# Pair 3's transposes moved from the matrix engine to the DMA queue, two others put ahead of stores, in a fused retention and bilinear feed-forward kernel

## The chip, the cores and the metric

The kernel runs on one core of one Trainium2 chip. The metric is the device time of one execution in microseconds (us). Times are medians over several executions, and each kernel is compared with the kernel before in runs on the same chip in the same batch. Only one execution of one experiment fell in the chip's "slow" state (named where it happens); all comparisons use fast runs.

## The reference

Two stages. First, retention (linear attention with a decay) over 8 batches, 8 heads, 576 positions and a head size of 64. Then a bilinear feed-forward on the 4608 tokens.

```python
scores = scale * np.matmul(q, k.transpose(0, 1, 3, 2))
gamma = 1.0 - 2.0 ** (-5.0 - np.arange(H))
Dmat = np.where(rel >= 0, gamma[:, None, None] ** rel, 0.0)
x = np.matmul(scores * Dmat, v)            # then (B, S, H*D) -> (4608, 512)
out = ((x @ w_a) * (x @ w_b)) @ w_out      # 512 -> 1536 -> 512
```

## The kernel before

The kernel interleaves the two stages by hand. The feed-forward runs in blocks of tokens: block 0 has 512, blocks 1 and 2 have 256, all others 512. Between its products a list called `todo` starts the pieces of the attention that a later block needs; the number in front is a place in the stream of products, counted in products of 512 columns. From the seventh 128-row tile on, the attention works on "pairs" of tiles (256 tokens), numbered 3 to 17: pair 3 is the first. A pair goes through these steps: `load_pair` (DMA in), `ahead` (GpSimd casts to bf16), a transpose of queries and keys, and a "stretch", in which TensorE makes the states (`kv`), the scores (`sc`) and the outputs (`o`).

All loads, all stores and all DMA transposes are issued by one engine, SyncE, in program order:

```python
def load_pair(n, which=(0, 1, 2)):
    ...
            nc.sync.dma_start(...)                 # two issues for each of q, k, v

def turn(n):                                       # transposes of a pair by DMA
    qkb = of(natural, n)[0]
    qkT = qkt_pool.tile([128, 2, 2, HP, 128], BF16, tag="qkT", name="qkT2")
    for w in (0, 1):                               # queries, then keys
        nc.sync.dma_start_transpose(
            qkT[:, w].rearrange("p k c s -> p (k c) s"), qkb[:, w])
    ...

def turned(n, part):                               # the same on TensorE, pair 3 only
    ...
    tp = ps_ffn.tile([128, HP, 128], BF16, tag="ab", name="tp2")
    for c in range(HP):                            # 4 transposes; called 4 times
        nc.tensor.transpose(tp[:, c, :], qkb[:, w, e0:e0 + 128], identity)
    copy = (nc.scalar.copy, nc.vector.tensor_copy)[kp]
    copy(of(transposed, n)[:, w, kp], tp)
```

The output of a block leaves through one of four SBUF buffers (`osb`). Blocks 1 and 2 have all their output copies on ScalarE, the same engine that copies `pa` out of PSUM and converts the states:

```python
o_pool = pool("osb", 4)
...
for u in range(n // 128):                          # in ffn_block(tb, tok0, n, runs)
    osb = o_pool.tile([128, DM], FP32, tag="osb", name="osb")
    ...                                            # po = hT x wo_sb, 12 products
    elif n == 256 or (u + part) % 2 == 0:
        nc.scalar.copy(osb[:, cols], po[:, 0:width])
    ...
    store(tok0 // 128 + u, cols, osb)              # nc.sync.dma_start
    pop()                                          # runs one deferred piece of work
```

The deferred pieces (`later`) are taken up one at a time by `pop()`, at fixed points of the feed-forward. They mask the scores and add the state sums on VectorE, and convert the states to bf16 on ScalarE. The schedule, as far as it matters here:

```python
warm(8, 512)                                       # fillers at the start
...
for n in (FIRST, FIRST + 1):                       # FIRST = 3
    load_pair(n)
load_pair(FIRST + 2, (Q, K))
...
todo += [(170, stretch, (3, None)), (197, stretch, (4, 3)),
         (236, stretch, (5, 4)), (266, open_alone, (5,)), ...
casts = {3: 116, 4: 116, 5: 141, 6: 200, 7: 250, 8: 330}
turns = {4: 116, 5: 145, 6: 240, 7: 338, 8: 345}
todo += [(156 + 3 * part, turned, (3, part)) for part in range(4)]
todo += [(116, load_pair, (5, (V,)))]
```

Of the kernel before, what the change touches and what calls it, by code (L numbers as in the profile page):

```python
# [10 lines left out]
FP32 = mybir.dt.float32  # L11
BF16 = mybir.dt.bfloat16
# [6 lines left out]
def kernel(  # L19
# [10 lines left out]
    nc = tc.nc  # L30

    B, H, S, D = q.shape
    DM = H * D
# [4 lines left out]
    HP = H // 2  # L38
# [8 lines left out]
    FIRST = 3  # L47
# [27 lines left out]
    qkt_pool = pool("qkt", 3)  # L75
# [46 lines left out]
    def half(i):  # L122
        return slice(64 * i, 64 * i + 64)
# [37 lines left out]
    Q, K, V = 0, 1, 2  # L161
# [311 lines left out]
            op=ALU.mult)  # L473
        natural[FIRST + n, "pair"] = (qkb, vb)

    def turned(n, part):

        qkb = of(natural, n)[0]
        if part == 0:
            transposed[FIRST + n, "pair"] = qkt_pool.tile(  # L480
                [128, 2, 2, HP, 128], BF16, tag="qkT", name="qkT2")
        w, kp = part // 2, part % 2
        tp = ps_ffn.tile([128, HP, 128], BF16, tag="ab", name="tp2")
        for c in range(HP):
            e0 = kp * DM + c * 128
            nc.tensor.transpose(tp[:, c, :], qkb[:, w, e0:e0 + 128], identity)
        copy = (nc.scalar.copy, nc.vector.tensor_copy)[kp]
        copy(of(transposed, n)[:, w, kp], tp)

    def turn(n):  # L490
        qkb = of(natural, n)[0]
        qkT = qkt_pool.tile([128, 2, 2, HP, 128], BF16, tag="qkT",
# [8 lines left out]
    def of(store, n):  # L501
        return store[FIRST + n, "pair"]
# [179 lines left out]
    def store(u, cols, osb):  # L682
        n, u = place(u // 2), u % 2
        for kp, r0, m, b, s0 in rows_of(n):
            rows = out[b * S + s0:b * S + s0 + m, cols]
            if kp != u:
                continue
            if n < FIRST:
                for par in (0, 1):
                    nc.sync.dma_start(rows[par::2], osb[half(par), cols])  # L690
            else:
                nc.sync.dma_start(rows, osb[r0:r0 + m, cols])

    begun = {}

    def ffn_begin(F):
# [13 lines left out]
    def ffn_block(tb, tok0, n, runs):  # L710
# [42 lines left out]
        for u in range(n // 128):  # L753
            final = tok0 + (u + 1) * 128 == NTOK
            osb = o_pool.tile([128, DM], FP32, tag="osb", name="osb")
            for part in range(2 if final else 1):
                cols = (slice(part * DM // 2, (part + 1) * DM // 2) if final
                        else slice(0, DM))
                po = ps_ffn.tile([128, 512], FP32, tag="ab", name="po")
                width = cols.stop - cols.start  # L760
                for F in range(NF):
                    nc.tensor.matmul(po[:, 0:width],  # L762
                                     hT[:, F, u * 128:(u + 1) * 128],
                                     wo_sb[:, F, cols],
                                     start=(F == 0), stop=(F == NF - 1))
                    if F in (2, 5, 8):
                        pop()
                    if F < NF - 1:
                        yield width / 512, F % 4 == 3
                if part:  # L770
                    mid = (cols.start + cols.stop) // 2
                    nc.scalar.copy(osb[:, cols.start:mid],
                                   po[:, 0:width // 2])
                    nc.vector.tensor_copy(osb[:, mid:cols.stop],
                                          po[:, width // 2:width])
                elif n == 256 or (u + part) % 2 == 0:
                    nc.scalar.copy(osb[:, cols], po[:, 0:width])  # L777
                else:
                    nc.vector.tensor_copy(osb[:, cols], po[:, 0:width])  # L779
                store(tok0 // 128 + u, cols, osb)  # L780
                pop()
                yield width / 512, True

# [4 lines left out]
    def warm(count, n):  # L788

        w = ps_ffn.tile([128, 512], FP32, tag="ab", name="w")  # L790
        for _ in range(count):
            nc.tensor.matmul(w[:, 0:n], ones[:, 0:128], ones[:, 0:n],  # L792
                             start=True, stop=True)

    W1, W2 = 128 * WCOLS[0], 128 * (WCOLS[0] + WCOLS[1])
    vector, pool_ = nc.vector, nc.gpsimd
    warm(8, 512)
    make_qs(qs_o, 0, 0, 512)
    for i in range(4):
        place_step(i)  # L800
# [67 lines left out]
        load_step(*STEPS[i], which)  # L868
    for n in (FIRST, FIRST + 1):
        load_pair(n)  # L870
    load_pair(FIRST + 2, (Q, K))



# [30 lines left out]
    def turn_step(i):  # L905
# [8 lines left out]
            (140, output_step, (5,))]  # L914
    todo += [(28 + 6 * step, pair_tables, (step,)) for step in range(13)]
    todo += [(170, stretch, (3, None)), (197, stretch, (4, 3)),
             (236, stretch, (5, 4)), (266, open_alone, (5,)),
             (270, close_outputs, (5,)), (336, stretch, (6, None)),
             (372, stretch, (7, 6)), (408, stretch, (8, 7))]
    for n in range(8, NP, 2):  # L920
# [4 lines left out]
    todo += [(starts[NP - 2] - 40, close_outputs, (NP - 1,))]  # L925
    placed = {args[0]: at for at, fn, args in todo if fn is stretch}
    casts = {3: 116, 4: 116, 5: 141, 6: 200, 7: 250, 8: 330}
    turns = {4: 116, 5: 145, 6: 240, 7: 338, 8: 345}
    loads = {7: 212, 8: 271, 9: 345.1, 10: 345.2}
    todo += [(145.1, load_pair, (6, (K,))),  # L930
             (145.2, load_pair, (6, (Q,))), (145.3, load_pair, (6, (V,)))]
    for n in range(9, NP):
        casts[n], turns[n] = placed[n] - 70, placed[n] - 38
    todo += [(156 + 3 * part, turned, (3, part)) for part in range(4)]
    for fn, places in ((ahead, casts), (turn, turns), (load_pair, loads)):
        todo += [(at, fn, (n,)) for n, at in places.items()]
    todo += [(116, load_pair, (5, (V,)))]
    todo.sort(key=lambda e: e[0])

    at = 0.0  # L940
# [40 lines left out]
```

## Time and profile before

| | before |
|---|---|
| time, first three runs | 330.65 us median (329.9 to 331.17) |
| span of the profiled execution | 328.6 us |
| TensorE busy | 322.2 us, 98% |
| granted clock, profiled execution | 1.000 |
| first product of block 0 / 1 / 2 / 3 | 17.69 / 52.86 / 71.52 / 90.45 us |

With an engine that is busy for 98% of the span, the useful question is not "how busy is it" but "where does it stand still, and for what". The last row of the table is the moments at which TensorE starts the first product of each block. (Line numbers: the scores are L587 in the kernel before and L573 in the changed one; the other lines shift likewise.)

### The profile page before, as it was taken

Reading aid. Unit: us, or ns where it says so; the run is one execution under the profiler, and the core shown is the slowest. Engines: PE = TensorE matmul, PEld = TensorE weight load, DVE = VectorE, ACT = ScalarE, POOL = GpSimd, SP = SyncE. Lnnn points to the kernel's source line nnn. Section 1 sums busy time; section 2 is a strip of 40 time slices with the busy share of each in tenths; the row PEclk is TensorE's granted clock in tenths of the full one; section 3 lists DMA queues with packets and bytes.
Section 4 is the critical chain, followed back from the end, with each engine's and each line's share of the span. In section 5 each row is a group of like instructions: output and inputs, shape, how many; then the busy total and the mean of one; then the engine's idle time right before and its main releaser. Section 6 shows DMA issues by size and latency. Waiting matters only on the chain.

```text
span 328.6 us, 8735 instructions
## 1 busy us (share of the span) xinstructions
PE 322.2 (98%) x3658; PEld 168.9 (51%) x3658; DVE 162.5 (49%) x291; ACT 128.9 (39%) x277; POOL 114.5 (35%) x146
## 2 busy tenths in 40 slices
PE   8999999999999999999999999999999999999995
PEld 4664467867544554545454545454445444444443
DVE  6744445665536673745274626562456245414421
ACT  7734743553435424533244323531333333213321
POOL 3960069820867185644074305360520000000000
PEclk9999999999999999999999999999999999999999
DMA  7999999989999999991799068935850510031013
GB/s 214 253 184 207 258 229 216 186 197 194 221 227 244 199 209 248 219 215 55 178 215 202 35 151 203 193 100 132 184 101 16 143 38 0 2 96 34 1 32 96
DMA packets 143175, 50.37 MB, mean 153 GB/s; under 512 B 124576, under 2 KB 138656, under 8 KB 143136
## 3 DMA queue, kind: packets, MB, share of 16 engines
q1 hardware_dynamic: 138384, 45.10, 62.8%
q0 software_dynamic: 4752, 4.72, 8.9%
q8 instruction: 28, 0.46, 0.6%
q14 instruction: 11, 0.09, 0.1%
HBM read 37.75 MB, written 9.44 MB: 144 GB/s over the span
## 4 chain that ended last, share of the span: by engine, by line
PE 92%; DMA 2%; POOL 2%; DVE 1%; SPq 1%; issue 1%; ACT 1%; POOLq 0%; ACTq 0%; DVEq 0%
PE po L762 27%; PE pb L743 27%; PE pa L728 26%; PE w L792 2%; PE o L613 1%; PE o L626 1%; DMA vf<-in_v_dram 1%; PE sc L587 1%; PE kv L360 1%; DMA qkT<-qkb 1%; PE kv L530 1%; PE tp L316 1%; PE pa L705 1%; PE o L421 1%; PE sc L331 1%
## 5 line engine op out<-in xcount | busy, mean ns | idle before, releaser
L748 DVE TENSOR_TENSOR hT<-ha,pb 128x512 bf16<-128x512 bf16 (+1 forms) x120 | 75.8, 633 | 99.1 <-PE pb L743 93.4
L736 ACT CAST ha<-pa 128x512 bf16<-128x512 f32 (+1 forms) x120 | 64.8, 542 | 120.4 <-PE pa L728 116.6
L743 PE MATMUL pb<-xT,wb_sb 128*128 128x512 bf16 (+1 forms) x480 | 111.5, 358 | 0.1
L728 PE MATMUL pa<-xT,wa_sb 128*128 128x512 bf16 (+1 forms) x468 | 108.8, 357 | 0.0
L762 PE MATMUL po<-wo_sb,hT 128*128 128x512 bf16 (+1 forms) x444 | 97.5, 374 | 0.4 <-issue 0.4
L743 PEld LDWEIGHTS <-wb_sb 128*128 128x128 bf16 x480 | 46.9, 98 | 46.6 <-issue 0.3
L728 PEld LDWEIGHTS <-wa_sb 128*128 128x128 bf16 x468 | 44.9, 98 | 44.3 <-issue 0.2
L762 PEld LDWEIGHTS <-hT 128*128 128x128 bf16 x444 | 42.2, 98 | 47.2 <-issue 0.5
L464 POOL CAST qkb<-qf 64x1024 bf16<-64x1024 f32 x15 | 15.4, 1030 | 82.8 <-DMA qf<-in_q_dram 80.6
L469 POOL TENSOR_TENSOR vb<-vf,vs 128x1024 bf16<-128x1024 f32 x15 | 28.5, 1901 | 11.7 <-DMA vf<-in_v_dram 8.7
L779 DVE COPY osb<-po 128x512 f32<-128x512 f32 (+1 forms) x16 | 10.8, 674 | 39.5 <-PE po L762 39.5
L777 ACT COPY osb<-po 128x512 f32<-128x512 f32 x20 | 11.7, 585 | 44.9 <-PE po L762 44.6
L636 DVE TENSOR_TENSOR xT<-o,qs 128x512 bf16<-128x512 f32 x30 | 19.5, 683 | 4.4 <-PE o L626 4.4
L550 DVE TENSOR_TENSOR sums<-kv,sums 128x256 f32<-128x256 f32 x46 | 19.5, 424 | 2.8 <-PE kv L530 0.8
L596 DVE TENSOR_TENSOR sT<-sc,mask 128x512 bf16<-128x512 f32 x30 | 19.5, 682 | 0.0
L468 POOL CAST qkb<-kf 64x512 bf16<-64x512 f32 x30 | 17.6, 614 | 0.9
L468 POOL CAST qkb<-qf 64x512 bf16<-64x512 f32 x30 | 17.6, 614 | 0.6
L464 POOL CAST qkb<-kf 64x1024 bf16<-64x1024 f32 x15 | 15.5, 1033 | 6.0 <-DMA kf<-in_k_dram 5.7
L554 ACT CAST states<-sums 64x512 bf16<-64x512 f32 x26 | 16.0, 617 | 0.3
L299 POOL CAST qkb<-kf 128x512 bf16<-128x512 f32 x5 | 3.1, 613 | 19.1 <-DMA kf<-in_k_dram 19.1
L792 PE MATMUL w<-ones 128*128 128x256 bf16 (+1 forms) x34 | 7.9, 361 | 1.5 <-DVE ones L197 1.5
L653 ACT COPY fence<-o 128x2 f32<-128x2 f32 x15 | 2.4, 161 | 15.8 <-PE o L613 15.8
(83 smaller groups left out, 163.0 us busy)
## 6 DMA issues: line engine op xcount, KB each, us to landing
qf<-in_q_dram SPq DMA_DIRECT2D x32, 256.0 KB, 4.8
kf<-in_k_dram SPq DMA_DIRECT2D x32, 256.0 KB, 5.2
vf<-in_v_dram SPq DMA_DIRECT2D x32, 256.0 KB, 5.2
out_dram<-osb SPq DMA_DIRECT2D x25, 256.0 KB, 2.2
out_dram<-osb SPq DMA_DIRECT2D x22, 128.0 KB, 2.4
wo_sb<-in_moe_w_out_dram POOLq DMA_DIRECT2D x3, 512.0 KB, 16.8
qf<-in_q_dram SPq DMA_DIRECT2D x8, 128.0 KB, 3.4
kf<-in_k_dram SPq DMA_DIRECT2D x8, 128.0 KB, 3.5
```

Source lines behind the costliest of these rows:

```text
L464: nc.gpsimd.tensor_copy(qkb[0:64, w], t[0:64])
L468: nc.gpsimd.tensor_copy(to[:, :, 1 - r], fro[:, :, r])
L469: nc.gpsimd.tensor_tensor(vb.rearrange("p (k h d) -> p k h d", k=2, h=H), vf.rearrange("p (k h d) -> p k h d", k=2, h=H), vs2[:, 2 if n in ...
L550: nc.vector.tensor_tensor(sums[:, i], own, prev, op=ALU.add)
L554: nc.scalar.copy(to(half(1 - r)), fro(half(r)))
L596: nc.vector.tensor_tensor(sT[:, on].rearrange("p c k s -> p (c k) s"), sc[:, on].rearrange("p c k s -> p (c k) s"), mask3.unsqueeze(1).to_ ...
L636: nc.vector.tensor_tensor(x_of(t0, 128).rearrange("p c (a s) -> p c a s", a=2), o[:, :, :, kp].rearrange("p a c s -> p c a s"), qs[:, :, s ...
L728: nc.tensor.matmul(pa[:, 0:n], wa_sb[:, c, fs], xT[:, c], start=(c == 0), stop=(c == NC - 1))
L736: nc.scalar.copy(ha[:, 0:n], pa[:, 0:n])
L743: nc.tensor.matmul(pb[:, 0:n], wb_sb[:, c, fs], xT[:, c], start=(c == 0), stop=(c == NC - 1))
L748: nc.vector.tensor_tensor(hT[:, F, 0:n], has[F][:, 0:n], pb[:, 0:n], op=ALU.mult)
L762: nc.tensor.matmul(po[:, 0:width], hT[:, F, u * 128:(u + 1) * 128], wo_sb[:, F, cols], start=(F == 0), stop=(F == NF - 1))
```

## The change

The intent is to take sixteen transposes out of TensorE's stream by giving pair 3's to the DMA queue, as all other pairs' are, and to have the transposes of pairs 4 and 5 issued before stores that nobody waits for. The stretch of pair 5 moves four products on, and 48 short fillers on two quadrants of the array take the place of three long ones at the start. The diff, cut:

```diff
-    def turned(n, part):
-        ...
+    held = []
+
+    def store_held():
+        while held:
+            store(*held.pop(0))
...
-                store(tok0 // 128 + u, cols, osb)
+                if tb == 0 and u > 1:
+                    held.append((u, cols, osb))
+                else:
+                    store(tok0 // 128 + u, cols, osb)
...
+    def warm_quads(count):          # 64-column matmuls on 64 x 64 quadrants in turn
+        ...
-    warm(8, 512)
+    for _ in range(3):
+        warm_quads(16)
+    warm(5, 512)
...
-    load_pair(FIRST + 2, (Q, K))
...
-             (236, stretch, (5, 4)), (266, open_alone, (5,)),
+             (240, stretch, (5, 4)), (266, open_alone, (5,)),
...
-    turns = {4: 116, 5: 145, 6: 240, 7: 338, 8: 345}
+    turns = {5: 145, 6: 240, 7: 338, 8: 345}
...
-    todo += [(156 + 3 * part, turned, (3, part)) for part in range(4)]
...
-    todo += [(116, load_pair, (5, (V,)))]
+    todo += [(116, turn, (3,)), (116, load_pair, (5, (Q,))),
+             (116, turn, (4,)), (116, load_pair, (5, (K, V))),
+             (145, store_held, ())]
```

More of the change, by code (lines that the diff above doesn't have):

```diff
@@ L474, in ahead @@
         natural[FIRST + n, "pair"] = (qkb, vb)
-    def turned(n, part):
-        qkb = of(natural, n)[0]
-        if part == 0:
-            transposed[FIRST + n, "pair"] = qkt_pool.tile(
-                [128, 2, 2, HP, 128], BF16, tag="qkT", name="qkT2")
-        w, kp = part // 2, part % 2
-        tp = ps_ffn.tile([128, HP, 128], BF16, tag="ab", name="tp2")
-        for c in range(HP):
-            e0 = kp * DM + c * 128
-            nc.tensor.transpose(tp[:, c, :], qkb[:, w, e0:e0 + 128], identity)
-        copy = (nc.scalar.copy, nc.vector.tensor_copy)[kp]
-        copy(of(transposed, n)[:, w, kp], tp)
     def turn(n):
@@ L793, in warm @@
                              start=True, stop=True)
+    def warm_quads(count):
+        w = ps_ffn.tile([128, 512], FP32, tag="ab", name="w4")
+        for i in range(count):
+            r = i % 2
+            nc.tensor.matmul(w[half(r), 0:64], ones[half(r), 0:64],
+                             ones[half(r), 0:64], start=True, stop=True)
     W1, W2 = 128 * WCOLS[0], 128 * (WCOLS[0] + WCOLS[1])
     vector, pool_ = nc.vector, nc.gpsimd
-    warm(8, 512)
+    for _ in range(3):
+        warm_quads(16)
+    warm(5, 512)
     make_qs(qs_o, 0, 0, 512)
```

## The prediction

> **What bounds the kernel now.** I read the page's busy shares first, then the chain of work that ended last, then TensorE's timeline between 53 and 81 us, the SyncE queue's timeline over the same stretch, and last the first 6 us.
>
> ```profile
> PE 322.2 (98%) x3658; PEld 168.9 (51%) x3658; DVE 162.5 (49%) x291; ACT 128.9 (39%) x277; POOL 114.5 (35%) x146
> PE 92%; DMA 2%; POOL 2%; DVE 1%; SPq 1%; issue 1%; ACT 1%; POOLq 0%; ACTq 0%; DVEq 0%
> ```
>
> TensorE is busy all the time and is 92% of the chain. So a saving counts only if it takes work or a wait out of TensorE's own stream, and TensorE executes its instructions in order: a wait in front of one matmul holds all that follow. The 8% that are not TensorE lie in the first 18 us and in one place near 77 us:
>
> ```profile
> 66.01 4.25 DMA vf<-in_v_dram
> ...
> 70.48 1.91 POOL vb L469
> 72.40 1.10 SPq L495
> ...
> 73.60 3.29 DMA qkT<-qkb
> ...
> 76.93 0.45 PE sc L587 x32
> ```
>
> Columns: start, length, what. The scores of pair 5 (L587) waited for a transpose by DMA, issued at 73.60 and landed 3.29 us later. The matmuls before it (L530, 32 at about 11.6 ns each) started at 76.23, so without the wait the scores would have started at about 76.5. It costs about 0.4 us. After it TensorE slips by another 0.6 us in the next four products (78.0 to 80.4), where VectorE has the state sums to add between its products and the four PSUM buffers are taken.
>
> The part that the change removes, in TensorE's timeline (start, length, what; overlapping lengths include the pipeline, so I go by starts):
>
> ```profile
> 57.67 0.39 PE L486 MATMUL tp<-identity,qkb 128*128 128x128 bf16 x4
> 57.90 0.60 PE L728 MATMUL pa<-xT,wa_sb 128*128 128x256 bf16 x4
> ...
> 59.96 0.45 PE L530 MATMUL kv<-vb,qkb 64*64 64x64 bf16 x32
> 60.23 0.44 PE L587 MATMUL sc<-qkT 64*64 64x64 bf16 x32
> 60.60 0.61 PE L728 MATMUL pa<-xT,wa_sb 128*128 128x256 bf16 x4
> ```
>
> A group of four transposes delays the next product by 0.22 us. The scores of pair 3 start at 60.23 with nothing to wait for, only 1.5 us after the last transpose.
>
> The SyncE queue, which issues every load, store and transpose in program order:
>
> ```profile
> 51.91 2.09 SPq L142 DMA_DIRECT2D vf<-in_v_dram  x2
> 54.10 2.49 SPq L142 DMA_DIRECT2D qf<-in_q_dram  x2
> 56.69 3.23 SPq L142 DMA_DIRECT2D kf<-in_k_dram  x2
> 60.02 0.74 SPq L690 DMA_DIRECT2D out_dram<-osb  x1
> ...
> 61.51 3.82 SPq L495 DMA_TRANSPOSE qkT<-qkb  x2
> 65.38 1.25 SPq L142 DMA_DIRECT2D vf<-in_v_dram  x2
> 66.74 5.35 SPq L690 DMA_DIRECT2D out_dram<-osb  x6
> 72.19 2.67 SPq L495 DMA_TRANSPOSE qkT<-qkb  x2
> ```
>
> It goes from issue to issue without a pause from 33 us on, about 1.1 us for each 256 KB load, and the page shows the DMA engines at nine tenths there. The queue is full: what stands in it lands some 4 to 6 us after its issue. Whoever puts a transfer on this queue has to look at when the queue gets to it.
>
> The start:
>
> ```profile
> 1.52 3.59 PE L792 MATMUL w<-ones 128*128 128x512 bf16 x8 [1.52 <-DVE ones L197]
> ...
> 4.91 1.06 PE L316 MATMUL tp<-identity,qkb 128*128 128x128 bf16 x8
> ```
>
> Eight fillers take 0.43 us each, twice the 0.216 us of the same size later on; the first transposes start when they end.
>
> **What the Trainium skill says.** (1) "TensorE: Matmul & The Clock Gate", Part 1: the clock stays at half until a free-running window of about 3.4 us has been busy. The trace agrees: fillers from 1.52 us run at half rate, the 256-column ones at 5.76 come down to 0.109 us. Since the window doesn't start with the kernel, the moment of the grant is partly chance. (2) Same page, Part 4: a transpose on TensorE lands in PSUM and needs a copy, and costs about 275 ns in a kernel. The copies are here (585 ns on ScalarE, 418 on VectorE), but the cost isn't: 0.22 us for four, 55 ns each. The measurement decides. (3) "DMA: Bandwidth & Descriptors", "Queues, rings and completion order": on each DMA engine descriptors are consumed in ring order. The trace agrees: landings on this queue follow the order of issue. (4) Same page, "Rules for kernel authors": a transpose next to ordinary DMAs needs nothing, so no extra wait is put between them.
>
> **The change part by part.**
>
> Pair 3 off TensorE. Sixteen transposes at 55 ns: 16 x 0.055 = 0.88 us less in TensorE's stream, all on the path. Two copies each on ScalarE and VectorE go too, in stretches where neither is late: nothing.
>
> Pair 3 onto the queue. The loads up to pair 4's values end their issue at 54.0 as before. Pair 5's queries and keys no longer follow; the first block's first store does: two issues of 0.69, 54.1 to 55.5. Then pair 3's transposes: queries 55.5 to 56.9, keys from 57.0. Their sources are long cast (GpSimd finished pair 3's keys at 51.4). Landing: pair 4's transpose, issued in the same place behind the same loads and stores, took 4.6 us from issue (61.51 to about 66.1). So the keys land at 57.0 + 4.6 = 61.6. TensorE, 0.88 us earlier, is at these scores at 60.23 - 0.88 = 59.35, for the stretch of pair 3 is left where it was. It must wait 61.6 - 59.35, about 2.2 us. This is the term I trust to decide the sign: 0.88 saved, 2.2 given back, so +1.35 net at this point.
>
> Pairs 4 and 5 ahead of stores. From 58.3: pair 5's queries (2.3) to 60.6, pair 4's transposes (2.7) to 63.3, landed by about 67; needed at 67.39 + 1.35 = 68.7: no wait. Then pair 5's keys and values (4.2) to 67.5, one store pair to 68.8, transpose of the queries to 70.2. The keys land at about 70, their casts take 1.03 + 1.17, so the second transpose is issued at about 72.2 and lands at about 75.5. Pair 5's stretch, four products (4 x 0.216 = 0.86 us) later and 1.35 us later from above, is at its scores at about 76.5 + 2.2 = 78.7. The wait of 0.4 us goes: -0.4. Half of this would have come from either part alone. The four products are only moved, not removed: 0. The sums that hold up TensorE by 0.6 us stand behind the stretch in the new place too, so I count 0.
>
> Fillers. Three of eight fillers (3 x 0.43 = 1.3 us) become 48 of 64 columns on two quadrants of the array in turn. On four quadrants at full clock the trace has 11.6 ns each (32 in 0.37 us), so on two about 23, at half clock up to 46: 1.1 to 2.2 us. The first transposes are between 0.2 us earlier and 0.9 later. What arrives by DMA at 7 to 14 us in the start sets much of the rest. Above all, whatever the start gives or costs up to about 2 us is swallowed by the wait at pair 3's scores, which ends by the DMA queue's clock. So 0.
>
> Sum: 330.65 - 0.88 + 2.2 - 0.4 = 331.6. I shade it to 331.4, since the landing is the soft number and has more room to be earlier than later.
>
> **Rivals.** (a) The transposes land sooner: two loads fewer stand in the queue, and where it wasn't full a transpose took 3.3 us. Then the keys land at 60.3, the wait is 0.95, and the sum is 330.3: no change. The full landing row (median 3.4 over all 28) speaks for it, the nine-tenths DMA at 54 to 62 us against it. (b) They land before 59.35: then the change saves 1.3 us, 329.3. It would need a latency of 2.3 us; I saw none so short. (c) The fillers matter: the clock comes a whole window later because short matmuls on half the array don't count as busy. Then up to 3.4 us run at half rate, 1.7 us lost, of which the wait at pair 3 hides most; at worst about 332.5. (d) The two added transposes (2.6 us of issue) push the whole queue back, and the later pairs wait: pair 7's last transpose landed at about 107.7 and is needed at 110.85, so 3 us of slack cover it, barely. If it doesn't, +0.3.
>
> **Range and chances.** The three runs before spread from 329.9 to 331.17, half a us either way. With the landing between 60.3 and 62.0 the sum runs from 330.3 to 332.0; with the scatter and the fillers I say 329.9 to 332.8. Two per cent is 6.6 us, and no part is that large in either direction: within 2% almost for sure, faster 0.01, slower 0.02.
>
> **What would show it.** In the chain of waits or TensorE's waits of the changed kernel: pair 3's scores idle on the landing of their transpose, at about 59.4, for 1 to 2.5 us (right), or no idle time there (wrong: rival b). Pair 5's scores no longer wait. TensorE's busy time falls by about a us. In the SyncE queue: pair 3's transposes at about 55.5, pair 5's at 69 to 72. First transposes between 4.7 and 5.9 us. If the time falls under 329.5, my latency for a transpose in the full queue is wrong; if it rises over 333, the fillers or the queue further down are.

## The result, and the profile after

| | before | after |
|---|---|---|
| median (lowest to highest), 4 runs each | 330.27 us (329.63 to 331.17) | 333.87 us (333.14 to 335.59) |
| span of the profiled execution | 328.6 us | 331.8 us |
| TensorE busy | 322.2 us | 319.7 us |
| first product of block 0 / 1 / 2 / 3 | 17.69 / 52.86 / 71.52 / 90.45 | 17.71 / 52.88 / 74.61 / 94.20 |

The ratio is 1.0114, 95% interval 1.0066 to 1.0163: slower by about 1.1%. That is within 2%, but above the range of the prediction. (Ratios here and below are the mean time of one kernel's fast runs over that of the other's fast runs of the same rounds, so not quite the ratio of the medians quoted.) Executions over 1.5% slower than the fastest of the same kernel are left out of the means.

The table locates most of it. In the profiled executions block 0 is as long as before, block 1 is 3.07 us longer (21.73 for 18.66), block 2 0.66 longer; from block 3 on the changed kernel is even 0.61 shorter. Part of that last figure is one pause of 0.40 us at 149.7 us in the profile before; of the other profiles only that of queue_alone (run 9) has one over 0.16 us at that point.

On the page of the changed kernel, two lines show where to look: the clock by slices of the span, and the chain of work that ended last.

```profile
PEclk9999999799999999999999999999999999999999
PE 78%; DMA 9%; SPq 6%; POOL 2%; issue 2%; ACT 1%; DVE 0%; POOLq 0%; ACTq 0%
```

The chain now leaves TensorE for 22% of the span in place of 8%. (That is no measure of the time lost: through one wait the chain changes over to the DMA queue and follows it back to the start.) And one digit of the clock, the eighth slice (58.1 to 66.4 us), is 7 where the page of before has 9 throughout. TensorE's timeline over that slice (start, length, what, and in brackets idle time and what ended it):

```profile
59.09 0.45 PE L516 MATMUL kv<-vb,qkb 64*64 64x64 bf16 x32
61.63 0.65 PE L573 MATMUL sc<-qkT 64*64 64x64 bf16 x32 [2.10 <-DMA qkT<-qkb]
62.21 1.04 PE L720 MATMUL pa<-xT,wa_sb 128*128 128x256 bf16 x4
...
65.33 0.60 PE L720 MATMUL pa<-xT,wa_sb 128*128 128x256 bf16 x4
```

There are two losses in these four lines. The first was predicted: pair 3's scores stand still for 2.10 us until their transposed keys land. The second was not: the four products that follow take 1.04 us, those at 65.33 take 0.60 (lengths include the pipeline; from start to start it is 0.213 us for one product against 0.109). The trace gives the granted clock by stretches; here busy time by engine, then the clock, for two stretches of 3.41 us (columns: stretch, length, busy us of PE, PEld, DVE, ACT, POOL with instructions, PEclk, DMA share, GB/s):

```profile
58.22:61.63 3.41, 1.31 (x41) 0.92 (x39) 0.84 (x2) 0.41 (x2) 2.88 (x3) 1.00 0.98 185
61.63:65.04 3.41, 3.41 (x46) 2.55 (x47) 0.80 (x3) 0.42 (x2) 0.69 (x1) 0.50 1.54 202
```

After the stretch with the wait in it, in which TensorE was busy for 1.31 of 3.41 us, the clock was halved for exactly one such stretch. From 61.63 to 65.33 TensorE took 3.70 us for the scores and sixteen products of 256 columns; at full clock that is 0.37 + 16 x 0.109 = 2.12, so about 1.6 us were lost. So block 1 adds up: -0.88 (the transposes) + 2.27 (the wait, start to start over the usual step) + 1.6 = 3.0 of 3.07.

The SyncE queue answers to the same view of before:

```profile
55.27 1.35 SPq L676 DMA_DIRECT2D out_dram<-osb  x2
56.73 2.91 SPq L481 DMA_TRANSPOSE qkT<-qkb  x2
...
61.11 3.17 SPq L481 DMA_TRANSPOSE qkT<-qkb  x2
...
68.34 1.72 SPq L676 DMA_DIRECT2D out_dram<-osb  x2
70.23 3.62 SPq L481 DMA_TRANSPOSE qkT<-qkb  x2
73.95 2.45 SPq L676 DMA_DIRECT2D out_dram<-osb  x4
```

Pair 3's transposes (56.73) come behind the first block's first store, those of pair 4 (61.11) and pair 5 (70.23) ahead of the held stores, which leave only at 73.95. The store at 68.34 is that of block 0's second output; pair 5's keys and values are now issued ahead of it. It matters below.

My theory at this point: the wait at pair 3's scores and the half clock that followed it are the whole loss. The rivals: the later stores and the moved stretch cost something that this profile hides; the fillers at the start cost something; or the fuller queue hurts later pairs.

### The profile page after: what moved, and what is told of

Its sections match the earlier page's. It is cut to its first block, busy times and chain, and to the rows that moved or that the text cites. A ratio compares the mean times of both kernels' runs of the same rounds, so it can differ in the third digit from the quotient of the medians.

```text
span 331.8 us, 8754 instructions
## 1 busy us (share of the span) xinstructions
PE 319.7 (96%) x3649; PEld 170.2 (51%) x3687; DVE 161.9 (49%) x289; ACT 128.3 (39%) x275; POOL 114.8 (35%) x146
## 4 chain that ended last, share of the span: by engine, by line
PE 78%; DMA 9%; SPq 6%; POOL 2%; issue 2%; ACT 1%; DVE 0%; POOLq 0%; ACTq 0%
PE po L754 25%; PE pa L720 24%; PE pb L735 24%; DMA wo_sb<-in_moe_w_out_dram 5%; SPq L153 4%; SPq L142 3%; DMA vf<-in_v_dram 2%; DMA qf<-in_q_dram 2%; PE o L599 2%; PE o L612 1%; PE sc L573 1%; PE kv L516 1%; DMA qkT<-qkb 1%; POOL qkb L464 1%; POOL vb L309 1%
## 5 line engine op out<-in xcount | busy, mean ns | idle before, releaser
L754 PE MATMUL po<-wo_sb,hT 128*128 128x512 bf16 (+1 forms) x429 | 94.8, 373 | 1.9 <-issue 1.4
L464 POOL CAST qkb<-qf 64x1024 bf16<-64x1024 f32 x15 | 15.5, 1031 | 87.2 <-DMA qf<-in_q_dram 79.3
L468 POOL CAST qkb<-qf 64x512 bf16<-64x512 f32 x30 | 17.7, 616 | 1.3 <-DMA qf<-in_q_dram 0.7
L468 POOL CAST qkb<-kf 64x512 bf16<-64x512 f32 x30 | 17.7, 616 | 0.9
L573 PE MATMUL sc<-qkT 64*64 64x64 bf16 x480 | 7.5, 198 | 2.1 <-DMA qkT<-qkb 2.1
L339 DVE TENSOR_TENSOR sT<-sc,mask_s 128x1024 bf16<-128x1024 f32 x6 | 7.3, 1222 | 2.9 <-PE sc L331 2.9
```

The source lines that it names most:

```text
L464: nc.gpsimd.tensor_copy(qkb[0:64, w], t[0:64])
L468: nc.gpsimd.tensor_copy(to[:, :, 1 - r], fro[:, :, r])
L754: nc.tensor.matmul(po[:, 0:width], hT[:, F, u * 128:(u + 1) * 128], wo_sb[:, F, cols], start=(F == 0), stop=(F == NF - 1))
```

## The experiments

Twelve kernels in three batches, each timed in five rounds. The kernel before had a median of 330.25 us (329.27 to 331.14, 11 runs), 330.43 (329.24 to 333.0, 11) and 329.82 (329.35 to 332.32, 11) in them. All were correct. The edits are shown as short diffs against the changed kernel ("after"), or against the kernel before where said.

| run | median us (lowest to highest, runs) | ratio to before, 95% | runs with a half-clock window |
|---|---|---|---|
| after_again | 333.69 (332.82 to 336.76, 6) | 1.0115, 1.0081 to 1.0148 | 3 of 6 |
| pair3_on_pe | 331.59 (330.44 to 333.14, 6) | 1.0044, 1.0018 to 1.0071 | 0 of 6 |
| fill_wait | 333.53 (332.58 to 333.97, 5) | 1.0095, 1.0075 to 1.0116 | 0 of 5 |
| turn3_early | 331.95 (331.45 to 332.38, 6) | 1.0049, 1.0031 to 1.0068 | 0 of 6 |
| stretch5_back | 333.09 (332.85 to 334.1, 6) | 1.0079, 1.0041 to 1.0117 | 3 of 6 |
| fillers_only | 331.47 (330.56 to 332.24, 6) | 1.0019, 0.9984 to 1.0055 | 0 of 6 |
| store1_first | 333.35 (332.58 to 334.63, 6) | 1.0081, 1.0044 to 1.0117 | 3 of 6 |
| all_mended | 333.07 (330.77 to 335.56, 6) | 1.0077, 1.0029 to 1.0124 | 2 of 6 |
| queue_alone | 333.80 (332.44 to 335.51, 6) | 1.0110, 1.0073 to 1.0146 | 3 of 6 |
| wait_only | 332.40 (331.47 to 335.74, the 5 fast ones; the slow one took 337.73) | 1.0098, 1.0048 to 1.0147 | 3 of 6, one of them slow |
| stretch3_later | 337.36 (335.2 to 338.05, 6) | 1.0209, 1.0174 to 1.0244 | 6 of 6 |
| all_mended2 | 330.18 (329.02 to 330.72, 6) | 0.9999, 0.9968 to 1.003 | 0 of 6 |

The last column is read from the mean clock that each run reports. One stretch of 3.41 us at half clock in some 332 lowers the mean by 0.5 x 3.41 / 332 = 0.005, so I read a mean at or below 0.995 as at least one such stretch. (The trace records the clock only from its first change on, so the slow first microseconds of every run don't enter into the mean. Where there is no profile, the reading is an inference; for four of the runs the trace itself shows the stretches.)

### 1. The changed kernel once more (after_again)

No edit. 

> The changed kernel, untouched, as the yardstick of this batch. Theory A (the wait at pair 3's scores plus one window of 3.4 us at half clock that this wait brings about): about 333.5 us, the scores of pair 3 at about 61.6 us after an idle of about 2.1 us, and in the trace the products right after them at about 0.21 us for 256 columns instead of 0.109, for 3.4 us. Rival B (the fillers of the start cost the time): the first product of the feed-forward part would have to start some us after 17.7 us. Rival C (the half clock is chance and has nothing to do with the wait): some runs without it, at about 331.9.

This run's profile shows why one profile isn't enough. The wait is there, the half clock is not, and something else has appeared:

```profile
62.22 0.45 PE L573 MATMUL sc<-qkT 64*64 64x64 bf16 x32 [2.20 <-DMA qkT<-qkb]
...
75.61 0.60 PE L735 MATMUL pb<-xT,wb_sb 128*128 128x256 bf16 x4 [0.63 <-ACT osb L769]
...
88.48 0.44 PE L599 MATMUL o<-qkT,states 64*64 64x64 bf16 x31 [0.42 <-ACT states L540]
```

And its clock over the stretch with the wait (the next stretch has 1.00 again):

```profile
58.25:61.66 3.41, 1.76 (x45) 1.32 (x43) 1.01 (x3) 0.74 (x2) 3.27 (x4) 1.00 1.04 193
```

Here the same wait fell across the border of two stretches of the clock's grid, so that TensorE was busy for 1.76 us in the first of them. Of the ten runs of this kernel in all (four after the prediction, six here), the six with a half-clock window average 334.6 us and the four without 333.2. One of the six (336.76, mean clock 0.990) must have had two such windows; the five with one average 334.2. So one window is worth 1.0 us by these runs and 1.6 by the trace above, and it happens in six of ten. So it is a cost, but not the whole rest: without it the kernel is still some 3 us behind.

The two new waits had been there in the first profile too, or were covered there. The line at 75.61 says that a product waits for ScalarE's copy into an output buffer; ScalarE itself waited for the buffer. There are four, used in turn: block 0 fills all four, block 1's first output takes the first again, and its second output, this copy, needs the one whose store was the second of block 0. That store stands behind pair 5's keys and values; it lands at 74.88 us here, at 71.90 before, and the copy starts at 74.98. (There was no slack to begin with: in the kernel before, ScalarE stood 0.29 us for this same store.) In the first profile the store landed at 74.33, but the half clock had shifted the work so that ScalarE was still converting states until 74.81: the wait was covered. The line at 88.48 says that pair 5's outputs wait for states that ScalarE has to convert. The conversions are popped one product later now that the stretch stands four products on, while the outputs stayed where they were (266).

### 2. Pair 3 back on TensorE, all else as changed (pair3_on_pe)

```diff
-    todo += [(116, turn, (3,)), (116, load_pair, (5, (Q,))),
+    todo += [(116, load_pair, (5, (Q,))),
...
+    todo += [(156 + 3 * part, turned, (3, part)) for part in range(4)]
```

> Everything of the change but the removed transposes: pair 3 is again transposed on TensorE, the fillers, the later stretch and the earlier transposes of pairs 4 and 5 stay. Theory A: no wait at pair 3's scores and no half clock, so within 0.7 us of the kernel before (329.8 to 331). Rival B (fillers) and a rival D (the reordered queue hurts by itself): stays near 333.

With 331.59 us, a little over the 329.8 to 331 expected, most of the loss is gone, and with it the half clock (none in six runs). So pair 3's move to the queue carries the larger part, about 0.7 of the 1.1%. Not all: +0.44% stays, an interval that excludes zero. From 15 us on its profile has no idle time over 0.42 us, and that one is the wait for states (0.63 us start to start over the usual step), which belongs to "four products on". The rest, under a us, may be the fillers (run 6) and where the start happens to fall: this execution stood 0.64 us for a cast at 14.2 us, and its first block began at 18.1 us, the one before at 17.7.

### 3. The wait filled with work that keeps the clock up (fill_wait)

```diff
 def matched(n):
+        if n == FIRST:
+            warm(10, 512)
```

Ten fillers of 0.216 us in front of pair 3's scores: TensorE is busy while it waits, and no wait is taken away. 

> The changed kernel with ten 512-column products on constants put ahead of pair 3's scores (10 x 0.216 = 2.16 us), so that TensorE is busy through the time in which it waited; the scores themselves still start when the transpose has landed, at about 61.7 us. Theory A with the idle time as the cause of the half clock: no slow window, the time falls by about 1.6 us against the changed kernel, to about 332. If the half clock is chance (rival C) or comes from elsewhere: no change, about 333.7.

The half clock is gone from all five runs, as expected. The time is not: 333.53 where I had expected 332. The fillers end just about as the keys land (idle 0.19 us before the scores), but then the wait for the output buffer opens:

```profile
61.81 0.45 PE L575 MATMUL sc<-qkT 64*64 64x64 bf16 x32 [0.19 <-DMA qkT<-qkb]
...
75.11 0.60 PE L737 MATMUL pb<-xT,wb_sb 128*128 128x256 bf16 x4 [0.53 <-ACT osb L771]
```

The expectation took the first profile for the kernel: it credited 1.6 us that only about half of the runs lose, and overlooked that the half clock had hidden another wait. Keeping the clock up is worth having only where the time behind it isn't owed to the next wait.

### 4. Pair 3's transposes ahead of pair 4's values and of the store (turn3_early)

```diff
-    for n in (FIRST, FIRST + 1):
-        load_pair(n)
+    load_pair(FIRST)
+    load_pair(FIRST + 1, (Q, K))
...
-                if tb == 0 and u > 1:
+                if tb == 0 and u != 1:
...
+    todo += [(116, ahead, (3,)), (116, turn, (3,)), (116, load_pair, (4, (V,))),
+             (116, ahead, (4,)), (116, store_held, ()),
+             (116, load_pair, (5, (Q,))), (116, turn, (4,)), (116, load_pair, (5, (K, V))),
```

> The changed kernel with pair 3's transposes put ahead of pair 4's values and of all stores in the SyncE queue, everything else kept. They should be issued at about 52 us and landed by about 57.7, before TensorE comes to the scores at 59.4. Theory A: no wait, no half clock, 16 transposes saved: about 329.5 to 330, that is 3.5 to 4 us under the changed kernel and some 0.5 us under the kernel before. Rivals B and D: still near 333.

The wait at pair 3's scores is gone (they start at 59.49), block 1 takes 18.72 us, and no run shows a half-clock window. But the kernel takes 331.95, not 329.5 to 330: what was behind in the queue is now late. Pair 4's scores wait 0.86 us for their transposes, and in block 2 ScalarE stands for an output buffer, and TensorE behind it (first fence ScalarE, second TensorE):

```profile
74.21 0.59 ACT L769 COPY osb<-po 128x512 f32<-128x512 f32 x1 [2.29 <-DMA out_dram<-osb]
```

```profile
74.85 0.60 PE L735 MATMUL pb<-xT,wb_sb 128*128 128x256 bf16 x4 [1.65 <-ACT osb L769]
```

This is the wait of run 1 in the open: the first line names a store as what ended ScalarE's idle time.

### 5. Pair 5's stretch back where it was (stretch5_back)

```diff
-             (240, stretch, (5, 4)), (266, open_alone, (5,)),
+             (236, stretch, (5, 4)), (266, open_alone, (5,)),
```

> The changed kernel with pair 5's stretch back at its old place, four products earlier; all else kept. In both profiles of the changed kernel the outputs of pair 5 (after its stretch) wait 0.63 us for the states that ScalarE converts; in the kernel before they don't. Theory E (the later stretch brings this wait, for its conversions now come a product later while the outputs have not moved): the 0.63 us are gone, and the mean of the runs falls by about 0.6 us. If the wait has another source (the wait at pair 3, the queue), it stays.

The wait for states is gone from the profile, and the median falls to 333.09. The intervals of this run and of the changed kernel overlap, so that the time alone doesn't prove the 0.63 us; the profile does show the wait to come with the four products and go with them. The wait at pair 3's scores is 2.77 us in this execution, the longest at this place in any profile, yet no half-clock stretch followed: TensorE was busy for 1.57 us in the stretch of the grid that held most of it.

### 6. The fillers alone, on the kernel before (fillers_only)

```diff
-    warm(8, 512)
+    for _ in range(3):
+        warm_quads(16)
+    warm(5, 512)
```

> The kernel before with the 48 short fillers alone. Rival B (the fillers cost part of the loss): 331 or more, the first product of the feed-forward part clearly after 17.7 us. Theory A: equal to the kernel before within 0.5 us, 329.8 to 330.8; the first transposes at about 5.05 us instead of 4.91.

The ratio is 1.0019 with an interval from 0.9984 to 1.0055: no effect that these rounds can tell from nought, and at most about half a per cent. In the changed kernel's first profile the 48 fillers took 1.42 us, 29.6 ns each, and the first transposes start at 5.05 us against 4.91 before. The profiled execution of fillers_only had a wait of 1.02 us for weights at 24.6 us that isn't in other profiles but one; I can't tell whether that is chance. Whether the fillers cost some half a us stays open.

### 7. Block 0's second store ahead of pair 5's keys and values (store1_first)

```diff
-             (116, turn, (4,)), (116, load_pair, (5, (K, V))),
+             (116, turn, (4,)), (121, load_pair, (5, (K, V))),
```

> The changed kernel with the store of the first block's second output ahead of pair 5's keys and values again in the SyncE queue (two stores issued some 4 us sooner). In the changed kernel's second profile ScalarE waits about 1.3 us for this store, because the output buffer that it empties is needed again at 73 us, and TensorE then stands 0.8 us. Theory F (a store put back in the queue holds the output buffer, and through ScalarE TensorE): this wait is gone, 0.5 to 0.8 us less than the changed kernel in runs without the half clock; the wait at pair 3 (2.3 us) stays. If the ScalarE wait has another cause, it stays.

The load of pair 5's keys and values now comes after that store. ScalarE's wait for the output buffer is gone in the profile (the store landed at 69.55). That alone proves little, since the half clock of this execution would have covered the wait, as in the first profile. wait_only (run 10) has the same order and no half clock near this place: there the store landed at 68.68, and ScalarE's copy started at 73.37 with no idle time before it. The median is 333.35 against 333.69, too small a difference for these intervals, and the two are from different batches. Its profile is a second view of the half clock. TensorE's wait for pair 3's transposes, then the two stretches of the clock's grid:

```profile
62.98 0.61 PE L573 MATMUL sc<-qkT 64*64 64x64 bf16 x32 [2.42 <-DMA qkT<-qkb]
```

```profile
59.66:63.07 3.41, 0.99 (x47) 0.64 (x48) 0.60 (x2) 0.37 (x1) 2.53 (x3) 1.00 0.96 173
63.07:66.48 3.41, 3.41 (x46) 2.49 (x47) 0.93 (x3) 0.55 (x2) 0.65 (x1) 0.50 1.81 216
```

### 8. All mends together (all_mended)

Run 4 with the old fillers, the stretch at 236, and pair 4's transposes ahead of the store and of pair 5's values:

```diff
-             (116, ahead, (4,)), (116, store_held, ()),
-             (116, load_pair, (5, (Q,))), (116, turn, (4,)), (116, load_pair, (5, (K, V))),
+             (116, ahead, (4,)), (116, turn, (4,)), (116, store_held, ()),
+             (116, load_pair, (5, (Q, K))), (121, load_pair, (5, (V,))),
```

> Pair 3 by DMA, but: its transposes ahead of pair 4's values, pair 4's next, then the first block's first store, pair 5's queries and keys, the second store, pair 5's values, pair 5's transposes, and the held stores last; pair 5's stretch at its old place and the eight long fillers of the kernel before. If the loss is the sum of the waits found so far (pair 3's transpose 2.3 us, half clock in some runs, the output buffer 0.8, the states 0.63), none of them is left here, the 0.88 us of transposes are saved: 329.2 to 330, under the kernel before by 0.3 to 1. If a wait comes up at pair 4's or 5's scores instead (the queue has no room for two more transposes of 1.3 us each), 330 to 331.

Block 1 is 17.81 us long, 0.85 less than before: the saving of 0.88 us for sixteen transposes is there when no wait eats it. But the kernel takes 333.07, a clear miss. The waits at pairs 3 and 4 are gone, an output buffer costs 1.49 us in block 2, and two new ones appear much later, at pair 7's scores (0.91 us) and at pair 9's:

```profile
136.18 0.45 PE L573 MATMUL sc<-qkT 64*64 64x64 bf16 x32 [2.57 <-DMA qkT<-qkb]
```

The same scores of the kernel before, with nothing to wait for:

```profile
132.49 0.50 PE L587 MATMUL sc<-qkT 64*64 64x64 bf16 x32
```

Pair 9's last transpose landed at 136.1 us here, at 130.37 before, 2.1 us ahead of its reader. SyncE's queue goes from issue to issue until about 145 us in the kernel before, so that whatever is added to it in the 50s pushes all of it back: pair 7's transposes were issued at 102.22 us before and at 105.35 in run 1. In the changed kernel TensorE had been delayed by about as much as the queue, which hid this.

### 9. Two transposes more on the queue, and nothing else (queue_alone)

On the kernel before, two DMA transposes of pair 3 into a spare buffer that nobody reads. All of the kernel's own work is left as it was, TensorE's transposes too.

```diff
+    def turn_unused():
+        spare = paired[2][Q].bitcast(BF16)
+        for w in (0, 1):
+            nc.sync.dma_start_transpose(
+                spare[:, 1024 * w:1024 * w + 1024]
+                .rearrange("p (k s) -> p k s", s=128),
+                of(natural, 3)[0][:, w])
...                                  # called at 116, between pair 3's casts and turn(4)
```

> The kernel before, pair 3 still transposed on TensorE and used from there, with two more transposes by DMA of pair 3 (into a staging buffer that is free then) whose results nobody reads, put in the SyncE queue just ahead of pair 4's transposes. Theory Q (the queue is full until about 140 us, so that two more transposes of 1.3 us push all that follows back by 2.6 us, whatever TensorE saves): waits at pair 4's scores (some 2 us) and at pair 5's, 332 to 333. If only the wait at pair 3's scores mattered, this kernel would take 330.3 as before.

333.80 us, ratio 1.0110: as slow as the whole change. The two spare transposes are issued at 62.71, just ahead of pair 4's, and TensorE waits for pair 4's keys:

```profile
67.19 0.44 PE L538 MATMUL kv<-vb,qkb 64*64 64x64 bf16 x32
70.72 0.45 PE L595 MATMUL sc<-qkT 64*64 64x64 bf16 x32 [3.09 <-DMA qkT<-qkb]
```

So two transposes on this queue cost about three us here (3.09 us of wait in this execution; the three runs without a half-clock window average 332.9, 2.6 over the kernel before), by what they push back, whoever reads them; and half of these runs show a half-clock window too. The wait at pair 5 that I had expected as well did not come. A pause of 1.05 us at 153.3 us, for which the profile shows no cause, lengthens this execution further. This wait is at another pair than in the changed kernel, since the spare ones stand at another place.

### 10. Only the wait left (wait_only)

Runs 3, 5 and 7 in one: fillers in the wait, the store first, the stretch at 236. If nothing but the wait at pair 3's scores is lost, this kernel shows it bare.

```diff
 def matched(n):
+        if n == FIRST:
+            warm(10, 512)
...
-             (240, stretch, (5, 4)), (266, open_alone, (5,)),
+             (236, stretch, (5, 4)), (266, open_alone, (5,)),
...
-             (116, turn, (4,)), (116, load_pair, (5, (K, V))),
+             (116, turn, (4,)), (121, load_pair, (5, (K, V))),
```

> The changed kernel with all other losses taken out: ten products on constants fill the wait at pair 3's scores (no half clock), the store of the second output goes ahead of pair 5's keys and values, and pair 5's stretch is at its old place. What is left is the wait itself: 330.3 - 0.9 + 2.4 = 331.8, between 331.3 and 332.3, and no run with a half-clock window. If the half clock has nothing to do with idle time, about half of the runs have it, as the changed kernel.

The three runs without a half-clock window (332.3, 331.47, 332.4) average 332.06, where 331.8 was expected. That no run would have a half-clock window was a miss: half of them have one (335.42, 335.74, and a slow one of 337.73), which is what I had said would speak against idle time as the cause. The profiled one of these tells why: it loses nothing at pair 3; pair 9's scores wait for the queue, and the half clock follows that. Where the other two had theirs no trace shows.

```profile
136.65 0.64 PE L575 MATMUL sc<-qkT 64*64 64x64 bf16 x32 [2.51 <-DMA qkT<-qkb]
```

```profile
133.12:136.54 3.42, 1.02 (x58) 0.58 (x56) 2.30 (x5) 0.32 (x2) 0.00 (x0) 1.00 1.20 121
136.54:139.95 3.41, 2.97 (x69) 1.83 (x71) 0.00 (x0) 0.38 (x1) 0.71 (x1) 0.50 1.36 218
```

### 11. The stretches of pairs 3 and 4 later (stretch3_later)

The transposes have time to land if pair 3's scores come later: the other plain way out of the wait.

```diff
-    todo += [(170, stretch, (3, None)), (197, stretch, (4, 3)),
+    todo += [(182, stretch, (3, None)), (204, stretch, (4, 3)),
```

> The changed kernel with pair 3's stretch twelve products later (three more pairs of products of 256 columns, 2.6 us) and pair 4's seven later, so that TensorE has work until the transpose has landed. Theory A: the wait at pair 3's scores is under 0.5 us and no run has a half-clock window; the wait for the output buffer and for pair 5's states may stay (0.8 and 0.63); 331 to 332. If a new wait for the states of pair 3 comes up instead, as pair 4's stretch follows too soon: above 332.

The wait at pair 3's scores is gone, and the kernel is the slowest of all, 337.36 us. It is the output buffer again. The store of block 0's second output is issued at 71.42 us (68.89 in after_again) and lands at 76.67, and ScalarE stands for it:

```profile
76.77 0.58 ACT L769 COPY osb<-po 128x512 f32<-128x512 f32 x1 [6.03 <-DMA out_dram<-osb]
```

The conversions of pair 4's states, popped before this copy in after_again, now come behind it and keep ScalarE until 79.3. TensorE waits for the one and then for the other:

```profile
77.41 0.60 PE L735 MATMUL pb<-xT,wb_sb 128*128 128x256 bf16 x4 [2.16 <-ACT osb L769]
...
79.67 0.78 PE L720 MATMUL pa<-xT,wa_sb 128*128 128x256 bf16 x4 [1.66 <-ACT ha L728]
```

All six runs have a half-clock window, and four of them, by a mean clock of 0.989 or 0.990, two. In the profiled execution one follows these waits (TensorE was busy for 0.87 us from 76.53 to 79.94). The other, from 18.50, has nothing to do with the edit, and adds something: in the 3.41 us ahead of it TensorE was busy for 3.03 us, of which only about 1.2 us were matmuls wider than one quadrant of 64 x 64. In the other kernels' profiles the same stretches of the start held 1.5 us or more of these, and no half clock followed. That would fit rival (c), that small matmuls count for less. But queue_alone speaks against it: its stretch from 69.22 us was busy for 1.75 us, only 1.05 of it wider than a quadrant, and no half clock followed. So the window at 18.50 stays unexplained.

### 12. All mended, with room made on the queue (all_mended2)

Run 8 with four changes that take the pressure off the queue: the stores of block 0's first two outputs issued by GpSimd's own queue, the first of them no longer held (the third and fourth still are), pair 7's transposes issued earlier, pair 10's load later.

```diff
-                    nc.sync.dma_start(rows[par::2], osb[half(par), cols])
+                    (nc.gpsimd if n == 0 else nc.sync).dma_start(
+                        rows[par::2], osb[half(par), cols])
...
-                if tb == 0 and u != 1:
+                if tb == 0 and u > 1:
...
-    turns = {5: 145, 6: 240, 7: 338, 8: 345}
-    loads = {7: 212, 8: 271, 9: 345.1, 10: 345.2}
+    turns = {5: 145, 6: 240, 7: 270.5, 8: 345}
+    loads = {7: 212, 8: 271, 9: 345.1, 10: 422.5}
...                                  # and no store_held at 116: it stays at 145
```

> The mended kernel of the batch before, with its three remaining waits taken out by order alone: the first block's two early stores go on GpSimd's own queue (the output buffer is then free in time: 1.65 us), pair 7's transposes go ahead of pair 8's loads (1.09 us), pair 10's loads after pair 9's transposes (2.75 us). Theory Q: the queue's order, not its load, made these waits, so they are gone and the saved transposes show: 328.5 to 330, under the kernel before. If the queue has no room at all, the waits come back elsewhere and the time stays at 331 or more.

Every wait told of above is gone; the longest idle time in TensorE's timeline from 20 us on is the one at pair 3's scores:

```profile
59.31 0.45 PE L573 MATMUL sc<-qkT 64*64 64x64 bf16 x32 [0.18 <-DMA qkT<-qkb]
```

The time is 330.18 us, ratio 0.9999: the 1.1% is won back, and no more. The profiled execution, the fastest of the six at 329.02, has a span of 327.3 us against 328.6, and block 1 is 0.54 us shorter than before; but the mean doesn't show the 0.88 us that the transposes cost. There is one profile for each kernel, so what takes it in the other five runs stays open.

One more build did not get as far: six output buffers in place of four, which would have removed that wait directly, don't fit in SBUF (12 KB per partition, 8.3 left).

## Why the prediction was wrong, point by point

The prediction's sum ended at 331.6 us; 333.87 were measured. What failed is not its main term, the wait at pair 3, but the terms that it set to nought or to a gain behind that wait: the clock after it, the stores that were put back, and the four products.

**Right: the wait, its place and its size.** The prediction had pair 3's keys land at 61.6 us; they landed at 61.59. Two errors cancelled there: the issue came later than I had it (58.23 for 57.0, since pair 4's values took 3.26 us to issue and not 2.09) and the flight was shorter (3.36 us for 4.6). It had TensorE at the scores at 59.35 and a net +1.35 at this point; the scores came at 61.63 against 60.23 before, +1.40. So the size is right by luck. Rivals (a) and (b), an earlier landing, are refuted, though (a) had the flight right (3.3 us).

**Right: 0.88 us for the sixteen transposes.** Block 1 of all_mended is 0.85 us shorter than before. And right in kind: pair 5's scores no longer wait. (The prediction set these 55 ns of delay against the page's 275 ns, which is the length of one transpose; see the last section. TensorE's busy time fell by 2.5 us where about one was forecast, but 38 matmul records are missing in that profile, so that I don't count this.)

**Wrong: the wait was counted at its length only.** The sum had 2.2 us for it. The prediction knew that the clock depends on how busy a window of some 3.4 us is, and used it for the fillers alone (rival c), not for the idle time that it had just computed. Its own sign for a time over 333 us named the fillers or the queue further down, not the clock behind the wait. Six of ten runs of the changed kernel have a window at half clock, worth 1.0 us by the runs and 1.6 by the trace; in the profiled one of them it follows the wait at once, and with the wait filled (fill_wait) no run of five has it. Over all, kernels whose profile shows an idle time of more than 2 us had such a window in 26 of 46 runs; the others, the kernel before among them, in 1 of 62 (for four runs of the kernel before no clock is on record). Not every one of these windows need be an echo of the wait at pair 3: pair 9's scores and the start have given one too.

**Wrong: "pairs 4 and 5 ahead of stores" as -0.4.** The step followed the readers of the transposes, and forgot who waits for the stores. It even had the store in its list of the queue ("one store pair to 68.8"; it was issued at 68.34 to 70.06), but not that a store which goes later keeps its output buffer longer. With four buffers ScalarE's copy waits for it, the copies out of PSUM that follow it on ScalarE come late, and with them TensorE. In after_again that cost 0.63 us of idle time, 0.8 start to start; turn3_early, in which TensorE comes earlier to the same point, shows 1.65.

**Wrong: "the four products are only moved, not removed: 0".** The work after the stretch, popped by place, moved with it; the outputs that need it did not. That is 0.63 us, start to start; the wait is in all seven profiles that have 240, and in none of the seven that have 236.

**Under-sized: rival (d), "+0.3".** I checked one late pair's slack and stopped. queue_alone shows 1.1%, some 3.6 us, from two more transposes on this queue, half-clock windows included. In the changed kernel this is mostly hidden, because TensorE is late by then as well; it comes out as soon as the other waits are mended (all_mended, wait_only).

**Not settled: the fillers.** Counted as 0; the interval of fillers_only runs from -0.2% to +0.55%.

The sum with what was measured, for a run without the half clock: -0.88 + 2.4 - 0.4 + 0.8 + 0.63 = +2.55 us, of 3.0 measured (333.2 against 330.2). With the half clock, 1.0 to 1.6 more. The remaining 0.4 to 0.5 us are of the size of the open question of the fillers and of the scatter of the start, and I can't assign them.

## What to carry to other kernels

A transfer is paid for by everything behind it on the same queue: before work is moved to a DMA queue, find out until when the queue is full and list the slack of every later reader, and of every buffer whose store moves back. An idle time of TensorE of 2 us or more should be counted with its echo, a following window of 3.4 us at half clock, with a chance rather than for sure; compare the mean clock of several runs, since one profile shows one draw. And when one wait is taken away, look in the next profile for the wait behind it: several stood in a row. Taking away the one at pair 3 by order (turn3_early) won back 1.7 us of some 3.5; mending the states or the output buffer alone moved the median by 0.6 and 0.3, less than the intervals can tell apart.

## What the Trainium skill lacked or had wrong

- "TensorE: Matmul & The Clock Gate", "Why this matters for your kernels", advises no idle gaps over about 3 us between bursts of matmuls, or one idle window brings back the half clock. Here less did it: idle times of 2.1 to 2.5 us (once 2.16 and 1.66 us in a row), when they left TensorE busy for 0.87 to 1.31 us of one window of the grid (3.41 us), were each followed by one window at half clock; windows with 1.57 us or more busy (waits of 2.77 and 3.09 us among them) were not, but for the unexplained one at the start of stretch3_later. The free-running window that the page describes in Part 1 fits this: what counts is where the gap falls in it.
- The same page, Part 4, puts a transpose on TensorE at about 275 ns in a kernel. That is how long one takes, and here the trace has 219 ns (ends are modelled). It lacks what a transpose costs in a stream of matmuls: sixteen of them, in groups of four between products, delayed TensorE by 55 ns each, 0.22 us for four; without them block 1 of all_mended was 0.85 us shorter.
- The same page, Part 1, gives about 25 ns as the least start-to-start time of small matmuls. It doesn't say there that this is for matmuls at one place of the array (Part 3 has those at different places overlap). 64-column matmuls on the four quadrants in turn started 8.1 ns apart on average here (32 within 0.25 us; the prediction's 11.6 ns counts the gap to the next product too); on two quadrants, at the start and at half clock, 26.7 ns.
- "DMA: Bandwidth & Descriptors", "DMA Transpose (X-bar)", has no time from issue to landing for a transpose from SBUF to SBUF (other sections of the page have a bandwidth and a count of sequencer cycles). Here one of 128 x 1024 bf16 elements took 1.2 to 3.3 us of SyncE's issue (median 1.3) and 3.0 to 6.8 us from issue to landing (median 3.6), over the 14 profiles.
